# Attention with decay and a gated convolution network on one core: the decay rows on other DMA queues, and a new order for the first half of the program

## The chip, the core and the metric

The kernel runs on one core of a Trainium2 chip. The metric is device time in microseconds, the median of several executions. One further execution was recorded by the hardware profiler; lines and durations come from it. A core has five engines that run side by side, each with an instruction queue of its own: PE (TensorE, matrix products; PEld is its loading of weights), DVE (VectorE), ACT (ScalarE), POOL (GpSimd) and SP (SyncE, which here only issues transfers). SP, ACT and POOL can each issue DMA transfers. An engine takes its instructions strictly in order and waits on semaphores for the others.

## The reference

Two steps follow each other. The first is causal attention with a forget gate, for 8 batches of 8 heads, 576 places, head size 64:

```python
scores = scale * np.matmul(q, k.transpose(0, 1, 3, 2))
cum = np.cumsum(np.log(np.clip(f, 0.0001, 1.0)), axis=-1)
decay = cum[:, :, :, None] - cum[:, :, None, :]
scores = np.where(causal, -1000000000.0, scores + decay)
attn = np.exp(scores - np.max(scores, axis=-1, keepdims=True))
attn = attn / (np.sum(attn, axis=-1, keepdims=True) + 1e-09)
return np.matmul(attn, v).astype(np.float32)
```

Its output, 576 x 512 for each batch, goes through a network with a gate from a convolution over three neighbouring places:

```python
h = np.maximum(x @ w_in, 0.0)                      # 512 -> 1024
conv_out += conv_w[k][None, None, :] * hp[:, k:k + S, :]   # k = 0, 1, 2
gate = 1.0 / (1.0 + np.exp(-conv_out))
return (h * gate @ w_out).astype(np.float32)       # 1024 -> 512
```

## The kernel before

**Tiling.** The work is cut into 16 half batches (hb, four heads each) for the attention and 8 batches (b) for the network. A half batch has two pairs of heads, i = 2 hb and 2 hb + 1. Half batches 0 and 1 are loaded plainly and turned on PE; from half batch 2 on a DMA transpose writes q and k into one of four ring buffers (`qk`).

**The decay on the scores.** Of each float32 number of q and k a bfloat16 half is used, and the other, even rows of a transposed buffer are free. The decay stands there: a row of -cum / scale beside rows of ones, so that the score product adds the difference itself. For that the decay is computed once (`kc`), written to a DRAM tile (`image`), and copied from there into the even rows of each ring buffer, one row on the q side (line 204, 4.5 KB) and two on the k side (line 205, 9 KB). Half batch 0 doesn't use the image: it adds the decay with two further products from `kc` (lines 317 and 319). From half batch 8 on, another function (`fill`) copies four rows at a time from SP. Ahead of the copy for half batches 2 to 7, a "clamp" on DVE (line 186) clears the even rows.

**Tasks.** The program is a list of 1054 named tasks. A string, `ORDER`, fixes the sequence in which they are emitted, and so the order of each engine's queue; where a task may go to several engines, the string names one after an @. The names that matter here:

- `ld`, `q`, `v`: loads of q and k, and of v, by SP. `wi`, `wo`: loads of the weights by SP; `wic`, `woc`: their cast to fp16. `va`: the cast of v.
- `dca`, `dcl`, `dcs`, `dck`: clip, logarithm, running sum, and the rows `kc` of the decay. `ki`: the image in DRAM (line 281, three DMAs). `cw`, `cwt`: the convolution's weights turned on PE, and their ratios on DVE.
- `tp hb.p.side`: q (side 0) or k (side 1) of a pair turned on PE; `cl`: the move out of PSUM (lines 172 and 174), or the clamp from half batch 2 on. `rw hb`: the copy of the image's rows.
- `sd i`, `so i.s`, `st hb`: scores on the diagonal, off it, and of the last 64 places, on PE; `ed`, `eo`, `et`: their exponentials on ACT (lines 355, 372, 334).
- `pv`: the product with v on PE; `n`, `m`: normalisation on DVE (405, 407); `t`, `tx`: the turn of the result on PE (416) and its copy (419).
- `f b.ff`: the network's first product on PE (431); `r`: relu on ACT (442); `c`, `d`: the convolution on DVE (448, 450); `a`: the gate's function on ACT (453); `g`: the gate on DVE (460); `o b.c`: the second product on PE (476); `e`, `s`: its copy and store.

**What the tasks share.** Four PSUM buffers of 128 x 1024 floats hold whatever PE writes; a task that writes one takes the buffer that has been free longest, and its reader on ACT or DVE gives it back. Each engine waits at the head of its queue, so a task that can't start holds everything behind it on that engine.

**Queues.** All transfers but the loads of `f` and `conv_w` and two of the row copies go through SP. SP issues them in order, and each waits on SP until its inputs are there.

Of the kernel before, what the change touches and what calls it, by code (L numbers as in the profile page):

```python
# [21 lines left out]
class Plan:  # L22
# [8 lines left out]
    def add(self, name, engines, after, fn, take=(), give=(), behind=()):  # L31
        assert name not in self.tasks
        self.tasks[name] = dict(engines=engines.split("/"), after=[a for a in after if a], fn=fn, take=list(take),
                                give=list(give), behind=[a for a in behind if a])
        return name
# [21 lines left out]
def kernel(  # L57
# [11 lines left out]
    nc = tc.nc  # L69
# [5 lines left out]
    BH = B * H  # L75
# [70 lines left out]
    add = plan.add  # L146
# [53 lines left out]
    def rows_of(hb, e="SP"):  # L200
        dma = {"SP": nc.sync, "ACT": nc.scalar}[e].dma_start
        h0 = 2 * PAIRS if hb == 0 else 0
        c = slice(hb * HH + h0, (hb + 1) * HH)
        dma(even_rows(hb, 0, 1, h0 * S, HS), image[0:1, 0, c, :].rearrange("j h s -> j (h s)"))
        dma(even_rows(hb, 1, 2, HS + h0 * S, 2 * HS), image[1:3, 1, c, :].rearrange("j h s -> j (h s)"))
# [73 lines left out]
    def decay_image(e):  # L279
        for j, a, h in ((0, 0, 0), (1, 1, 0), (2, 1, 1)):  # L280
            {"SP": nc.sync, "ACT": nc.scalar}[e].dma_start(image[j, a], kc[BH * h:BH * (h + 1)])
# [232 lines left out]
    def stage_cast(w, j, e):  # L514
# [5 lines left out]
        {"ACT": nc.scalar.copy, "POOL": nc.gpsimd.tensor_copy, "DVE": nc.vector.tensor_copy}[e](dst, ob)  # L520

    add("cw", "PE", [], conv_weights, take=["ps"])
    add("cwt", "DVE", ["cw"], conv_ratios, give=[("ps", "cw")])
    for x in range(0):
        add(f"wu{x}", "PE", [], lambda x=x: warm_up(f"wu{x}"), take=["ps"])
        add(f"wd{x}", "PE", [], lambda: None, behind=[f"wu{x}"], give=[("ps", f"wu{x}")])
    add("zc", "SP", [], constants)
    add("dca", "DVE", [], lambda: nc.vector.tensor_scalar(fsb, fsb, 1e-4, 1.0, op0=ALU.max, op1=ALU.min))
    add("dcl", "ACT", ["dca"], decay_log)
    add("dcs", "DVE", ["dcl"], decay_sum)  # L530
    add("dck", "DVE", ["dcs"], decay_rows)
    add("ki", "ACT/SP", ["dck"], decay_image)
    for w in ("wi", "wo"):
        for j in range(4):
            add(f"{w}{j}", "SP", [], lambda w=w, j=j: stage(w, j), take=["ob"])
            add(f"{w}c{j}", "POOL/ACT/DVE", [f"{w}{j}"], lambda e, w=w, j=j: stage_cast(w, j, e), give=[("ob", f"{w}{j}")])

    for hb in range(NHB):
        b = hb // 2
        was = hb - RING  # L540
        old = [f"st{was}"] + [f"sd{2 * was + y}" for y in range(2)] + [
            f"so{2 * was + y}.{s}" for y in range(2) for s in range(2)] if was >= 0 else []
        if hb < NPL:
            parts = [(p, side) for p in range(2) for side in range(2)]
# [13 lines left out]
            if hb == 0:  # L558
                ready = [["dck"] + [f"cl0.{p}.{side}" for side in range(2)] for p in range(2)]
                if PAIRS < 2:  # L560
                    add("rw0", "SP", ["cl0.1.0", "cl0.1.1", "ki"] + ([] if PAIRS else ["cl0.0.0", "cl0.0.1"]), lambda: rows_of(0))
                    ready = [ready[p] if p < PAIRS else ["rw0"] for p in range(2)]
            else:
                add(f"rw{hb}", "ACT/SP", [f"cl{hb}.{p}.{side}" for p, side in parts] + ["ki"], lambda e, hb=hb: rows_of(hb, e))
                ready = [[f"rw{hb}"]] * 2
# [127 lines left out]
```

## Time and profile before

| | |
|---|---|
| median of 3 executions | 245.96 us (245.56 to 246.7) |
| profiled execution | 247.66 us |
| its span, first to last instruction | 245.9 us |
| granted TensorE clock, mean | 0.999 |
| instructions in the span | 6391 |
| read from HBM, written to HBM | 21.11 MB, 10.17 MB |

The busy shares and the chain of waits are shown with the prediction. A row of a time line gives start and length in microseconds, the engine ("SPq" or "ACTq" is a DMA being issued by that engine's queue), the line of the kernel, the operation, and the tile written and the tiles read; in brackets stands how long the engine was idle before, and what ended that.

### The profile page before, as it was taken

Reading aid. Unit: us, or ns where it says so; the run is one execution under the profiler, and the core shown is the slowest. Engines: PE = TensorE matmul, PEld = TensorE weight load, DVE = VectorE, ACT = ScalarE, POOL = GpSimd, SP = SyncE. Lnnn points to the kernel's source line nnn. Section 1 sums busy time; section 2 is a strip of 40 time slices with the busy share of each in tenths; the row PEclk is TensorE's granted clock in tenths of the full one; section 3 lists DMA queues with packets and bytes.
Section 4 is the critical chain, followed back from the end, with each engine's and each line's share of the span. In section 5 each row is a group of like instructions: output and inputs, shape, how many; then the busy total and the mean of one; then the engine's idle time right before and its main releaser. Section 6 shows DMA issues by size and latency. Waiting matters only on the chain.

```text
span 245.9 us, 6391 instructions
## 1 busy us (share of the span) xinstructions
PE 229.1 (93%) x2627; PEld 146.5 (60%) x2627; DVE 205.7 (84%) x323; ACT 207.2 (84%) x278; POOL 52.6 (21%) x77
## 2 busy tenths in 40 slices
PE   0899899959999999999999999999999999999992
PEld 0778676537655776666556865685576557444440
DVE  5626329899999899999999988996999889999951
ACT  2748695999999889999999999999988997698452
POOL 8020430004240030004130481156303131000000
PEclk9999999999999999999999999999999999999999
DMA  6999799999999899999989999929999780551426
GB/s 202 329 154 231 242 189 206 219 201 325 225 203 191 198 196 219 234 301 212 234 248 249 177 191 283 263 48 187 272 245 197 185 192 4 129 176 50 171 87 213
DMA packets 120280, 49.68 MB, mean 202 GB/s; under 512 B 109863, under 2 KB 110375, under 8 KB 120251
## 3 DMA queue, kind: packets, MB, share of 16 engines
q1 hardware_dynamic: 120073, 48.94, 89.1%
q8 instruction: 20, 0.33, 0.6%
q10 hardware_dynamic: 178, 0.34, 0.5%
q14 instruction: 9, 0.07, 0.1%
HBM read 21.11 MB, written 10.17 MB: 127 GB/s over the span
## 4 chain that ended last, share of the span: by engine, by line
PE 79%; DVE 7%; DMA 5%; ACT 5%; issue 1%; SPq 1%; ACTq 0%; DVEq 0%
PE ps L476 25%; PE ps L431 24%; PE ps L314 15%; PE ps L391 7%; DMA qk<-image 3%; DMA u<-in_f_dram 2%; PE ps L396 2%; PE ps L416 2%; PE ps L322 2%; ACT qk L172 2%; DVE xm L407 2%; DVE u L448 1%; DVE u L450 1%; PE ps L317 1%; PE ps L319 1%
## 5 line engine op out<-in xcount | busy, mean ns | idle before, releaser
L431 PE MATMUL ps<-xt,w_in_f 128*128 128x512 f16 (+1 forms) x512 | 70.1, 287 | 0.4 <-DVE xt L419 0.4
L372 ACT ACTIVATE pp<-ps 128x1024 f16<-128x1024 f32 x64 | 64.6, 1030 | 4.1 <-PE ps L314 2.3
L476 PE MATMUL ps<-w_out_f,hg 128*128 128x512 f16 x288 | 66.8, 380 | 0.0
L314 PE MATMUL ps<-qk 128*128 128x128 bf16 (+2 forms) x576 | 64.8, 242 | 1.3 <-ACT pp L355 0.7
L448 DVE SCALAR_TENSOR_TENSOR u<-ht,cwt 128x576 f32<-128x576 f16 x64 | 54.0, 860 | 3.9 <-ACT ht L442 3.6
L453 ACT ACTIVATE hg<-u,cw 128x576 f16<-128x576 f32 x64 | 48.6, 781 | 6.1 <-DVE u L450 6.0
L450 DVE SCALAR_TENSOR_TENSOR u<-ht,cwt,u 128x576 f32<-128x576 f16 x64 | 52.9, 841 | 0.5
L431 PEld LDWEIGHTS <-w_in_f 128*128 128x128 f16 x512 | 34.3, 98 | 28.7 <-issue 0.5
L314 PEld LDWEIGHTS <-qk 128*128 128x128 bf16 x576 | 39.7, 98 | 19.5 <-issue 3.5
L442 ACT ACTIVATE ht<-ps 128x576 f16<-128x576 f32 x64 | 40.9, 661 | 6.4 <-PE ps L431 3.0
L476 PEld LDWEIGHTS <-hg 128*128 128x128 f16 x288 | 26.9, 98 | 28.9
L460 DVE SCALAR_TENSOR_TENSOR hg<-hg,ht 128x576 f16<-128x576 f16 x51 | 38.8, 773 | 0.5 <-ACT hg L453 0.5
L358 POOL TENSOR_SCALAR_AFFINE_SELECT pp<-pd 128x1024 f16<-128x1024 f32 x16 | 19.7, 1245 | 54.2 <-ACT pd L355 54.2
L391 PE MATMUL ps<-va,pp 128*128 128x65 f16 x640 | 24.8, 193 | 1.7 <-DVE va L219 1.7
L391 PEld LDWEIGHTS <-pp 128*128 128x128 f16 x640 | 22.6, 97 | 4.2 <-DVE va L219 2.0
L407 DVE TENSOR_TENSOR xm<-ps,rc 128x896 f16<-128x896 f32 (+1 forms) x32 | 23.9, 752 | 0.5
L355 ACT ACTIVATE pp<-ps 128x1024 f16<-128x1024 f32 x16 | 16.5, 1034 | 5.8 <-PE ps L314 3.3
L355 ACT ACTIVATE pd<-ps 128x1024 f32<-128x1024 f32 x16 | 16.2, 1023 | 1.2 <-PE ps L314 0.5
L219 POOL CAST va<-vf 128x1024 f16<-128x1024 f32 x8 | 9.9, 1233 | 32.6 <-DVE u L448 18.3
L322 PE MATMUL ps<-mask,ident 128*128 128x512 bf16 (+1 forms) x40 | 14.8, 370 | 1.4 <-ACT pp L372 0.8
L405 DVE RECIPROCAL rc<-ps 128x14 f32<-128x14 f32 (+1 forms) x32 | 6.7, 209 | 10.1 <-PE ps L396 4.9
L481 ACT COPY ob<-ps 128x1024 f32<-128x1024 f32 (+1 forms) x14 | 12.9, 918 | 0.3 <-issue 0.2
(83 smaller groups left out, 180.2 us busy)
## 6 DMA issues: line engine op xcount, KB each, us to landing
vf<-in_v_dram SPq DMA_DIRECT2D x32, 256.0 KB
out_dram<-ob SPq DMA_DIRECT2D x14, 512.0 KB
qk<-blank SPq DMA_DIRECT2D x8, 432.0 KB
ob<-in_moe_w_in_dram SPq DMA_DIRECT2D x4, 512.0 KB
ob<-in_moe_w_out_dram SPq DMA_DIRECT2D x4, 512.0 KB
out_dram<-ob SPq DMA_DIRECT2D x6, 256.0 KB
vf<-in_v_dram SPq DMA_DIRECT2D x8, 128.0 KB
qk<-blank SPq DMA_DIRECT2D x8, 108.0 KB
```

What stands on the lines that cost most here:

```text
L314: nc.tensor.matmul(o, tk[:, h * S + k0:h * S + k0 + 128], tq[:, h * S + q0:h * S + q0 + n], start=first, stop=last and not by_matmul(hb, h))
L355: nc.scalar.activation(o, ps_of(f"sd{i}").rearrange("p (s c) -> p s c", s=2), AF.Exp, scale=SCALE)
L372: nc.scalar.activation(pair(i)[:, s, 512:1536], ps_of(f"so{i}.{s}"), AF.Exp, scale=SCALE)
L391: nc.tensor.matmul(ps[:, c:c + D + 1], block(hb, h, m, n), va[:, h, m, 0:D + 1], start=(m == 0), stop=(m == n))
L407: nc.vector.tensor_tensor(xm[:, CUT * D * u:CUT * D * u + nj * k * D].rearrange("p (j x d) -> p j x d", x=k, d=D), got[:, :, :, 0:D], r.un ...
L431: nc.tensor.matmul(ps[:, t0:t1], w_in_f16[:, cc, 128 * ff:128 * (ff + 1)], xt[:, cc // 2, x:x + t1 - t0], start=(cc == 0), stop=(cc == NCC ...
L442: nc.scalar.activation(ht_of(b, ff)[:, 2:2 + S], ps_of(f"f{b}.{ff}")[:, 0:S], AF.Relu, scale=1.0 if (b, ff) in LATE else 0.5)
L448: nc.vector.scalar_tensor_tensor(u, ht[:, 1:1 + S], cwt[:, ff, 0:1], ht[:, 2:2 + S], op0=ALU.mult, op1=ALU.add)
L450: nc.vector.scalar_tensor_tensor(u, ht[:, 3:3 + S], cwt[:, ff, 1:2], u, op0=ALU.mult, op1=ALU.add)
L453: nc.scalar.activation(hg_of(b, ff), u_t[slot[f"c{b}.{ff}", "u"]], AF.Sigmoid if (b, ff) in LATE else AF.Tanh, scale=cw[:, ff, 1:2])
L460: nc.vector.scalar_tensor_tensor(hv, hv, 1.0, ht_of(b, ff)[:, 2:2 + S], op0=ALU.add, op1=ALU.mult)
L476: nc.tensor.matmul(ps[:, 512 * (c % 2):512 * (c % 2 + 1)], w, w_out_f16[:, ff, :], start=(ff == 0), stop=(ff == NFF - 1))
```

## The change

It has two parts.

**Engines.** `decay_image` and `rows_of` may now be issued by POOL as well, and the order names the issuer: the image by POOL (before by SP), the rows of half batches 1 and 3 by ACT (before by SP), those of 2, 4, 5, 6 and 7 by POOL (before 4 and 5 by ACT, the others by SP). Some casts and copies change their engine as well:

| tasks | before | now |
|---|---|---|
| va0.0, va6.0 | POOL | DVE |
| va4.0 | ACT | DVE |
| wic0, wic2, wic3 | POOL | DVE |
| e0.1 | ACT | DVE |
| va1.1, va2.0, tx0, tx4 | DVE | ACT |
| va3.0, va3.1, va5.1, va7.1, va8.0 | ACT | POOL |
| va4.1 | DVE | POOL |
| cl1.0.0 / cl1.0.1 | ACT / DVE | DVE / ACT |

**Order.** The first 500 of the 1054 places of `ORDER` are in a new sequence; from place 501 (`va9.0`) on it is word for word as before. SP's own loads keep their sequence; those tasks that left SP are simply gone from it.

```diff
-dca cw ld0 ld1 ld0.0.0 tp0.0.0 dcl ld0.1.0 ld0.0.1 tp0.0.1 tp0.1.0 v0.0 ld0.1.1 ld1.0.1 ld1.0.0 dcs dck v0.1 v0.2 v0.3 v0.4 va0.0@POOL ki@SP
...
+dca cw dcl ld0 ld1 ld0.0.0 ld0.1.0 tp0.0.0 ld0.0.1 tp0.0.1 v0.0 ld0.1.1 cwt ld1.0.1 dcs cl0.0.1@ACT tp0.1.0 dck ld1.0.0 cl0.0.0@ACT v0.1 ki@POOL
...
     def rows_of(hb, e="SP"):
-        dma = {"SP": nc.sync, "ACT": nc.scalar}[e].dma_start
+        dma = {"SP": nc.sync, "ACT": nc.scalar, "POOL": nc.gpsimd}[e].dma_start
...
     def decay_image(e):
         for j, a, h in ((0, 0, 0), (1, 1, 0), (2, 1, 1)):
-            {"SP": nc.sync, "ACT": nc.scalar}[e].dma_start(image[j, a], kc[BH * h:BH * (h + 1)])
+            {"SP": nc.sync, "ACT": nc.scalar, "POOL": nc.gpsimd}[e].dma_start(image[j, a], kc[BH * h:BH * (h + 1)])
...
-    add("ki", "ACT/SP", ["dck"], decay_image)
+    add("ki", "ACT/SP/POOL", ["dck"], decay_image)
...
-                add(f"rw{hb}", "ACT/SP", [f"cl{hb}.{p}.{side}" for p, side in parts] + ["ki"], lambda e, hb=hb: rows_of(hb, e))
+                add(f"rw{hb}", "ACT/SP/POOL", [f"cl{hb}.{p}.{side}" for p, side in parts] + ["ki"], lambda e, hb=hb: rows_of(hb, e))
...
-                add(f"rw{hb}", "ACT/SP", [f"cl{hb}.{side}" for side in range(2)] + ["ki"], lambda e, hb=hb: rows_of(hb, e))
+                add(f"rw{hb}", "ACT/SP/POOL", [f"cl{hb}.{side}" for side in range(2)] + ["ki"], lambda e, hb=hb: rows_of(hb, e))
```

What this does to the queues is seen at three places. First ACT, from the first exponential on, before (qk_85 and qk_86 are the ring buffers of half batches 0 and 1, pp_95 to pp_98 take the exponentials of pairs; L172 is the move of a turned q or k, L355 and L372 exponentials):

```order
L355 ACTIVATE pp_95<-ps_131 128x2x512
L372 ACTIVATE pp_95<-ps_132 128x1024
L372 ACTIVATE pp_95<-ps_131 128x1024
L172 ACTIVATE qk_86<-ps_129,lim 128x1152
L355 ACTIVATE pp_96<-ps_132 128x2x512
L172 ACTIVATE qk_86<-ps_129,lim 128x1152
L372 ACTIVATE pp_96<-ps_130 128x1024
```

The same place of ACT now:

```order
L355 ACTIVATE pp_95<-ps_131 128x2x512
L172 ACTIVATE qk_86<-ps_132,lim 128x1152 x2
L204 DMA qk_86<-image 1x2304
L205 DMA qk_86<-image 2x2304
L372 ACTIVATE pp_96<-ps_130 128x1024
L355 ACTIVATE pp_96<-ps_129 128x2x512
L372 ACTIVATE pp_96<-ps_131 128x1024
L372 ACTIVATE pp_95<-ps_132 128x1024
L372 ACTIVATE pp_95<-ps_130 128x1024
```

Both moves of half batch 1 now stand ahead of the five large exponentials of half batch 0 that are left, and its row copy, which waits for them and for DVE's share of the moves, stands in the middle of ACT's queue.

Second SP, from half batch 2's second transpose on, before (ob_125 to ob_128 take the four parts of the first weight, qk_88 is half batch 3's buffer):

```order
L180 DMA_TRANSPOSE qk_87<-in_q_dram 128x2304
L512 DMA ob_125<-in_moe_w_in_dram 128x2x512
L204 DMA qk_86<-image 1x2304
L205 DMA qk_86<-image 2x2304
L512 DMA ob_126<-in_moe_w_in_dram 128x2x512
L512 DMA ob_127<-in_moe_w_in_dram 128x2x512
L512 DMA ob_128<-in_moe_w_in_dram 128x2x512
L204 DMA qk_87<-image 1x2304
L205 DMA qk_87<-image 2x2304
L180 DMA_TRANSPOSE qk_88<-in_q_dram 128x2304
```

Third POOL, from its first task after the fills on, as it is now:

```order
L281 DMA image<-kc 64x576 x3
L219 CAST va_92<-vf_89 128x4x4x64
L221 CAST va_91<-vf_89 64x4x64
L204 DMA qk_87<-image 1x16x144
L205 DMA qk_87<-image 2x2304
L520 CAST w_in_f_69<-ob_125 128x2x512
L221 CAST va_93<-vf_90 64x4x64
L219 CAST va_94<-vf_90 128x4x4x64
L221 CAST va_94<-vf_90 64x4x64
L204 DMA qk_85<-image 1x16x144
L205 DMA qk_85<-image 2x2304
```

On SP the row copies between the weights, each of which waited for a move or a clamp, are gone. On POOL the copies of half batch 2 and, further down, of half batch 4 stand among the casts of v and of the weights; the one-row copy is built there as 16 pieces of 144 numbers.

2 lines of the change are left out of this document (1 added, 1 removed).

## The prediction

> **What bounds the kernel now.** I read the page first: the busy shares and the chain that ended last.
>
> ```profile
> PE 229.1 (93%) x2627; PEld 146.5 (60%) x2627; DVE 205.7 (84%) x323; ACT 207.2 (84%) x278; POOL 52.6 (21%) x77
> PE 79%; DVE 7%; DMA 5%; ACT 5%; issue 1%; SPq 1%; ACTq 0%; DVEq 0%
> ```
>
> PE is the bound, but a share is a mean over stages. So next I read the busy time of each engine in stretches (start:end, length, then PE, PEld, DVE, ACT, POOL, the granted clock, DMA share, GB/s).
>
> ```profile
> 6.75:16.00 9.25, 8.58 (x73) 7.71 (x73) 5.58 (x12) 5.68 (x5) 0.00 (x0) 1.00 1.02 279
> 16.00:27.00 11.00, 11.00 (x136) 8.56 (x135) 4.72 (x5) 8.80 (x9) 2.53 (x4) 1.00 0.89 177
> 27.00:40.00 13.00, 11.72 (x204) 8.95 (x201) 5.70 (x11) 9.20 (x11) 3.98 (x4) 1.00 1.10 219
> 40.00:50.00 10.00, 9.27 (x82) 5.40 (x80) 9.03 (x13) 8.68 (x13) 0.39 (x1) 1.00 1.16 231
> 50.00:60.00 10.00, 7.43 (x145) 5.76 (x147) 9.97 (x17) 9.65 (x15) 1.52 (x1) 1.00 1.12 265
> 60.00:120.00 60.00, 59.77 (x719) 38.38 (x718) 57.93 (x86) 57.57 (x79) 9.97 (x9) 1.00 1.09 221
> 120.00:220.00 100.00, 100.00 (x1170) 61.98 (x1168) 92.57 (x136) 92.44 (x128) 28.78 (x28) 1.00 0.84 190
> ```
>
> From 60 to 220 us PE is idle for 0.23 us. Between 27 and 60 it is idle for 13 - 11.72 = 1.28, 0.73 and 2.57 us, together 4.6. The order is unchanged from its 501st place on, and that place lies in the stretch in which PE is full. So the change can win at most about what PE loses before 60 us, and a lead won there is kept to the end as long as DVE and ACT, themselves at 96% from 60 to 120 us, carry it.
>
> What does PE wait for between 16 and 52 us? The time line of ACT (start, length, line, tiles; in brackets the idle time ahead and who ended it) shows two engines that feed each other through four PSUM buffers:
>
> ```profile
> 17.76 1.02 ACT L372 ACTIVATE pp<-ps 128x1024 f16<-128x1024 f32 x1 [0.62 <-PE ps L319]
> 19.58 1.02 ACT L372 ACTIVATE pp<-ps 128x1024 f16<-128x1024 f32 x1 [0.79 <-PE ps L319]
> 20.50 1.30 ACT L172 ACTIVATE qk<-ps,lim 128x1152 uint16<-128x1152 uint16 x1
> 25.48 1.02 ACT L372 ACTIVATE pp<-ps 128x1024 f16<-128x1024 f32 x1 [0.29 <-PE ps L319]
> 26.83 0.38 ACT L334 ACTIVATE pt<-ps 128x256 f16<-128x256 f32 x1 [0.33 <-PE ps L319]
> 28.71 1.02 ACT L355 ACTIVATE pp<-ps 128x1024 f16<-128x1024 f32 x1 [1.49 <-PE ps L314]
> 36.08 1.02 ACT L372 ACTIVATE pp<-ps 128x1024 f16<-128x1024 f32 x1 [0.41 <-PE ps L314]
> 38.25 1.02 ACT L355 ACTIVATE pp<-ps 128x1024 f16<-128x1024 f32 x1 [1.15 <-PE ps L314]
> 40.26 0.65 ACT L442 ACTIVATE ht<-ps 128x576 f16<-128x576 f32 x1 [0.98 <-PE ps L431]
> 41.67 0.65 ACT L442 ACTIVATE ht<-ps 128x576 f16<-128x576 f32 x1 [0.77 <-PE ps L431]
> 49.22 0.65 ACT L442 ACTIVATE ht<-ps 128x576 f16<-128x576 f32 x1 [0.30 <-DVE hg L460]
> ```
>
> The ten gaps add up to 7.1 us. Each buffer of scores needs 1.02 us of ACT and is held until then, so a gap of ACT is lost and comes back as PE's wait for a buffer. The early stage is bound by how well ACT is fed; that is what the new order must change.
>
> **The DMA edits.** SP keeps its other transfers in their order. It loses the image's three and two each for half batches 1, 2, 3, 6 and 7; what they cost now is the time in which SP waits for a clamp with weights queued behind it, and their landing:
>
> ```profile
> 24.46 0.69 SPq L205 DMA_DIRECT2D qk<-image  x1
> 27.10 0.59 SPq L205 DMA_DIRECT2D qk<-image  x1
> 27.10 6.63 DMA qk<-image
> 27.63 0.38 PE L322 MATMUL ps<-mask,ident 128*128 128x512 bf16 x1
> ```
>
> The rows of half batch 1 are issued until 25.15 and used at 27.63 without a wait: at most 2.5 us. Those of half batch 2, behind three weight loads, are issued until 27.69 and landed at 33.73: 6.0 us. PE waits for them at 33.7 with 0.15 us or less, so on their own they are worth nearly nothing. The weights and the next transposes are issued earlier, by the image's three issues at least; DMA is at 0.89 to 1.16 of its time from 16 us on, so they land perhaps 1 us earlier. I cost that at nothing, because the clamps of half batch 3 wait on DVE behind the first transposed outputs anyway.
>
> The Trainium skill, "DMA: Bandwidth & Descriptors", section "Issuing engines are not separate DMA queues", says that transfers issued from several engines end on the same 16 engines, so that spreading them saves only issue time. By that rule half batch 2 would still need something like the 6.0 us; the sum is the same by either, as the rows are wanted about 9 us after their clamp (below).
>
> The price of a row DMA on ACT depends on whether ACT is working when it is issued:
>
> ```profile
> 53.19 1.03 ACT L355 ACTIVATE pp<-ps 128x1024 f16<-128x1024 f32 x1
> 53.51 0.23 ACTq L204 DMA_DIRECT2D qk<-image  x1
> 53.78 0.66 ACTq L205 DMA_DIRECT2D qk<-image  x1
> ```
>
> Those two were issued under a running activation: nothing. Half batch 3 on ACT falls into such a full place: nothing. Half batch 1 does not, since it waits for the move just ahead of it on ACT: 0.23 + 0.66 = 0.9 us of ACT uncovered. No row shows a DMA issued by POOL. Its 13 issues are bounded by 0.23 us, the cheapest issue on a queue, and by POOL's longest cast here, 1.5 us; I take 1 us each, nearer to the casts, as POOL must do work for it. That is 13 us on an engine that is idle for 79% of the span; it shows only where a row lands late (a rival below).
>
> **The order, up to 27 us.** On DVE the seven small instructions of the convolution ratios now stand ahead of the scan.
>
> ```profile
> 10.55 0.76 DVE L276 SCALAR_TENSOR_TENSOR kc<-u,kc 64x576 bf16<-64x576 f32 x1
> 11.34 0.18 DVE L299 COPY cw<-ps 128x24 f32<-128x24 f32 x1
> 12.50 0.17 DVE L306 TENSOR_TENSOR cwt<-cw,cwt 128x8 f32<-128x8 f32 x1
> 19.88 0.38 PE L322 MATMUL ps<-mask,ident 128*128 128x512 bf16 x1
> 21.65 1.17 PE L166 MATMUL ps<-ident_b,hg 128*128 128x128 bf16 x18
> ```
>
> They take 1.3 us, of which some 0.7 fill DVE's wait for the logarithm, so the decay rows come at about 11.9 instead of 11.3. The first scores need them, and need the two moves of ACT that end at about 12.5: hidden, and without that cover it would be 0.6 us. Scores of pair 0 then end at 15.9 as before.
>
> Behind them PE now runs the transposes of half batch 1 (0.6 us each, half of the 1.17) to 17.1, scores of pair 1 (19.88 to 21.65, 1.8 us) to 18.9, two more transposes to 20.05. ACT does ed0 (to 17.1) and one move of 1.30 (to 18.45), and its next in order is the move of the last transpose: **idle 1.6 us**, and then the uncovered row DMA, **0.9**. From 22.3 on ACT has the five large exponentials left of half batch 0 and those of pairs 2 and 3 queued without a gap: PE is ahead of it by then, and half batch 1's rows are wanted at 25.3, 3.0 us after their issue, against the 2.5 above.
>
> **27 to 52 us.** PE stays ahead of ACT: st2 and so4.0 now stand ahead of f0.0, and so4.0, so4.1 and ed4 keep ACT busy where it had gaps of 0.98 and 0.77. ACT's relu takes 0.65 us, a group of f0 about 1.0 on PE (f0.0 and f0.1 stand ahead of the gaps of 0.98 and 0.77 above), so where two relus follow each other some 0.3 are left, twice at most: **0.5**. ACT's idle time becomes 1.6 + 0.9 + 0.5 = 3.0 us for 7.1.
>
> Against it stands work that changes engines, priced by these:
>
> ```profile
> 26.82 1.04 POOL L219 CAST va<-vf 128x1024 f16<-128x1024 f32 x1
> 38.76 0.76 DVE L419 COPY xt<-ps 128x1152 f16<-128x1152 f16 x1 [0.46 <-PE ps L416]
> 50.50 0.69 DVE L219 CAST va<-vf 128x1024 f16<-128x1024 f32 x1
> 51.57 1.06 ACT L219 CAST va<-vf 128x1024 f16<-128x1024 f32 x1
> 59.83 1.12 ACT L419 COPY xt<-ps 128x1152 f16<-128x1152 f16 x1
> 78.35 1.00 ACT L481 COPY ob<-ps 128x1024 f32<-128x1024 f32 x1
> ```
>
> ACT takes tx0 (1.12) and va1.1 (a 256-column piece, 0.38 as at 26.83); va2.0 comes and va3.0 goes at 1.06 each. **ACT's lead at 52 us: 7.1 - 3.0 - 1.5 = 2.6 us.**
>
> DVE takes va0.0 and three weight casts, all before 40 us, where it is idle for 7.3 of 13 us. From the first convolution on it gains 0.3 (f0.0 ready that much earlier), 0.69 (va2.0 goes) and a part of the 0.97 us that it is idle from 40 to 50: **DVE's lead at 52 us: between 1.0 and 2.0, and I take 1.3**, as it must still follow ACT's relus.
>
> **52 us to the end of the change.** All three are full here. ACT gets lighter (va3.1, va4.0, va5.1 and e0.1 go, tx4 comes). DVE gets va4.0 and va6.0 (0.69 each) and e0.1 (1.00, if as on ACT) for tx4 (0.76) and va4.1: +1.3 to +1.6, against 60 - 57.93 = 2.1 us of idle time from 60 to 120 us, which cover it; without that cover it would eat the whole lead of DVE.
>
> The sum therefore lies between DVE's 1.3 and ACT's 2.6. PE follows whichever is later in each place; I take the middle, **1.9 us**. The profiled execution took 247.66 us (span 245.9) and would take 245.8; it is 1.7 above the median of 245.96, and I take the same 1.9 off the median: **244.1 us**.
>
> **Rivals.** (0.5% is about what a measurement of this kernel can tell from no change, 1.2 us: 244.7 to 247.2.)
>
> *The lead is spent on DVE: 245.9.* DVE has 0.03 us free from 50 to 60 us and takes more work than it gives. If its lead at 52 us is 1.0 and the extra 1.3 falls into its full places, nothing is left: 245.96 + 0.3 - 0.3. For it: DVE's 96%; against: the 2.1 us of gaps. Range 245.2 to 246.9.
>
> *PE loses almost nothing before 60 us: 241.9.* Of its 4.6 us idle 0.5 stays. For it: the order was changed at every place where PE waits; against: ACT, which works 36.4 - 7.1 = 29.3 us between 16.1 and 52.5, would have to lose no more than 1.5 us there with its new work, and the two waits of 1.6 and 0.9 are in its order.
>
> *Rows issued by POOL land late: slower, 247.6.* One mechanism: the rows of half batches 4 and 5 wait on POOL behind casts and issue slowly. Those of half batch 4 can be issued when their clamp ends, at about 53 us, and are used where PE had them before:
>
> ```profile
> 60.41 0.39 PE L322 MATMUL ps<-mask,ident 128*128 128x512 bf16 x1
> 58.34 1.52 POOL L520 CAST w_out_f<-ob 128x1024 f16<-128x1024 f32 x1 [13.32 <-DMA ob<-in_moe_w_out_dram]
> ```
>
> That leaves about 7 us; the slowest row DMA above needs 6.0, and half batch 2's rows have some 9. From 7 us on each further microsecond costs one; from 9 the lead is gone; at 10.5 the time is 244.1 + 3.5 = 247.6. For it: a POOL cast took 1.52 us at 58 us beside a full DVE and 1.04 at 26.8, so POOL is slowed by half there. Against: even 1.5 us for each of two issues and 2.5 to land make 5.5.
>
> The Trainium skill, "SBUF — State Buffer", section "SBUF: two separate sides", speaks against the change: descriptors of a DMA issued by GpSimd cannot be written while DVE runs an instruction in a two-port mode, and a transfer of about 620 ns alone took about 3100 ns beside such a copy. By it the two issues would be an estimated 6.2 us and the rows about 1.7 us late. I give it no more than the rival's chance, since the slowed cast is the only row here that agrees with it.
>
> **How the numbers follow.** Forecast (243.3 to 244.7): 0.48. Lead spent on DVE: 0.27. Nearly all of PE's idle time gone: 0.12. Late rows: 0.13. The range from 242.0 to 247.2 takes in the forecast, the first rival, half of the second and the mild part of the last. Faster by over 0.5%: 0.48 + 0.12 less the edge, 0.58; within: 0.28; slower: 0.14.
>
> **What would show it.** Right: ACT's gaps between 16 and 52 us add up to about 3 us, with one of some 1.6 at 18.5 and one at 21.4; PE's idle time from 27 to 60 us falls from 4.6 to about 2.7; f0.7 and sd9 start about 2 us earlier; PE is full from 60 us on. Wrong: PE or ACT waiting for the image after 40 us (the rows from POOL), DVE gaps that vanish while PE has new waits for DVE between 60 and 120 us, or a first exponential of half batch 1 that waits for rows issued by ACT.

## The result and the profile after

| | before | changed |
|---|---|---|
| median | 246.33 us (4 runs, 245.56 to 249.16) | 252.45 us (4 runs, 252.16 to 253.84) |
| profiled execution | 247.66 us | 252.5 us |
| its span | 245.9 us | 250.8 us |
| granted TensorE clock, mean | 0.999 | 0.989 |

The changed kernel is **slower**: ratio 1.0251, 95% interval [1.0215, 1.0286], 6.1 us. The forecast was 244.1 us, the range 242.0 to 247.2. (The kernel of before has a fourth execution here, of 249.16 us, which moves its median from 245.96 to 246.33.)

The page of the changed kernel has the same busy PE and a shorter share of it in the chain that ended last: 68% where it was 79%, and DVE 12% where it was 7%.

```profile
PE 229.1 (91%) x2627; PEld 145.9 (58%) x2627; DVE 211.3 (84%) x325; ACT 206.0 (82%) x275; POOL 60.0 (24%) x91
PE 68%; DVE 12%; DMA 7%; ACT 6%; issue 2%; SPq 1%; ACTq 1%; DVEq 0%
```

Busy time by stretch of the changed kernel (start:end, length, then PE, PEld, DVE, ACT, POOL, granted clock, DMA share, GB/s):

```profile
6.75:16.00 9.25, 8.23 (x91) 7.52 (x92) 6.11 (x13) 6.79 (x7) 1.85 (x4) 1.00 1.19 303
16.00:27.00 11.00, 10.46 (x119) 7.77 (x118) 5.30 (x6) 8.37 (x9) 3.36 (x5) 1.00 1.07 254
27.00:40.00 13.00, 12.92 (x220) 9.97 (x220) 7.51 (x15) 12.17 (x16) 0.00 (x0) 1.00 1.23 213
40.00:50.00 10.00, 8.47 (x93) 5.22 (x92) 9.86 (x13) 8.83 (x14) 3.15 (x3) 1.00 1.28 203
50.00:60.00 10.00, 8.14 (x155) 5.98 (x152) 9.82 (x18) 8.91 (x12) 2.06 (x3) 1.00 1.13 261
60.00:70.00 10.00, 7.38 (x69) 4.22 (x67) 10.00 (x10) 6.79 (x10) 6.12 (x7) 1.00 1.06 195
70.00:80.00 10.00, 9.92 (x91) 6.22 (x91) 9.19 (x14) 8.70 (x13) 0.51 (x1) 0.83 1.07 205
120.00:140.00 20.00, 18.56 (x188) 10.67 (x186) 19.89 (x28) 17.54 (x26) 4.89 (x5) 1.00 0.88 211
140.00:220.00 80.00, 80.00 (x977) 50.34 (x974) 73.11 (x110) 72.96 (x101) 24.91 (x25) 1.00 0.78 177
```

PE's idle time up to 60 us, stretch by stretch, is 1.02, 0.54, 0.08, 1.53 and 1.86 us, together 5.0; before it was 0.67, 0, 1.28, 0.73 and 2.57, together 5.25. So **nearly nothing was won there**. From 27 to 60 us, the stretch of the forecast, it fell from 4.6 to 3.5 us and not to 2.7, and 0.54 us came up ahead of it. New losses stand where PE had been full: 2.62 us from 60 to 70, a clock of 0.83 from 70 to 80 (17% of 10 us, 1.7 us), and 1.44 us from 120 to 140.

PE's waits of the changed kernel, summed (us in total, times, longest):

```profile
PE ps L322 <- ACT ht L442: 2.7, 1, 2.7
PE ps L314 <- DMA qk<-image: 2.6, 3, 1.1
PE ps L314 <- ACT ht L442: 1.8, 3, 0.8
```

The second row is the rows of the image, for which PE waited 0.15 us before. The three waits on PE's time line, one each for half batches 1, 3 and 4:

```profile
24.63 0.40 PE L314 MATMUL ps<-qk 128*128 128x128 bf16 x4 [0.55 <-DMA qk<-image]
45.61 0.38 PE L314 MATMUL ps<-qk 128*128 128x128 bf16 x4 [1.09 <-DMA qk<-image]
59.23 0.40 PE L314 MATMUL ps<-qk 128*128 128x128 bf16 x4 [0.95 <-DMA qk<-image]
```

The first row of the summed waits is one event. Rows of POOL, DVE, ACT and PE around it, in the changed kernel:

```profile
60.40 0.81 DVE L448 SCALAR_TENSOR_TENSOR u<-ht,cwt 128x576 f32<-128x576 f16 x1
...
63.57 0.64 POOL L221 CAST va<-vf 64x256 f16<-64x256 f32 x1 [1.51 <-DMA vf<-in_v_dram]
64.15 2.03 POOL L520 CAST w_out_f<-ob 128x1024 f16<-128x1024 f32 x2
66.13 1.04 POOL L219 CAST va<-vf 128x1024 f16<-128x1024 f32 x1
67.18 1.50 POOL L520 CAST w_out_f<-ob 128x1024 f16<-128x1024 f32 x1
...
63.94 3.84 DVE L448 SCALAR_TENSOR_TENSOR u<-ht,cwt 128x576 f32<-128x576 f16 x1
67.70 2.25 DVE L460 SCALAR_TENSOR_TENSOR hg<-hg,ht 128x576 f16<-128x576 f16 x2
...
69.38 0.65 ACT L442 ACTIVATE ht<-ps 128x576 f16<-128x576 f32 x1 [2.82 <-DVE hg L460]
...
70.08 0.27 PE L322 MATMUL ps<-mask,ident 128*128 128x256 bf16 x1 [2.70 <-ACT ht L442]
72.22 0.63 PE L322 MATMUL ps<-mask,ident 128*128 128x512 bf16 x1
```

Five casts follow each other on POOL without a break from 63.57 to 68.68. The DVE instruction that begins at 63.94 takes 3.84 us; the same form took 0.81 at 60.40. ACT waits for the gate behind it, PE for ACT, and then PE runs at half rate: the product of 0.38 us takes 0.63 at 72.22. An idle time of that length doesn't always bring the half rate: in the kernel e7 below PE was idle for 3.24 us at the same place, and the clock column stayed at 1.00.

The loss between 120 and 140 us stands just behind the 500th place, where the order is as before:

```profile
124.77 3.17 POOL L358 TENSOR_SCALAR_AFFINE_SELECT pp<-pd 128x1024 f16<-128x1024 f32 x2
...
125.45 3.10 DVE L450 SCALAR_TENSOR_TENSOR u<-ht,cwt,u 128x576 f32<-128x576 f16 x2
128.47 0.75 DVE L460 SCALAR_TENSOR_TENSOR hg<-hg,ht 128x576 f16<-128x576 f16 x1
...
132.89 0.65 ACT L442 ACTIVATE ht<-ps 128x576 f16<-128x576 f32 x1 [2.07 <-DVE hg L460]
```

**The sum of the two spans.** PE's idle time up to 60 us -0.2, from 60 to 80 +2.6, from 80 to 120 -0.2, from 120 to 140 +1.4, the clock +1.7; the last copy starts 5.2 us before the end where it started 4.1 before it, +1.1. And the profiled execution of before had a slow start: -1.6, from these rows of PE (before, then changed):

```profile
12.89 0.31 PE L314 MATMUL ps<-qk 128*128 128x128 bf16 x1
13.00 0.31 PE L317 MATMUL ps<-sel_k,kc 128*128 128x128 bf16 x1
```

```profile
13.13 0.22 PE L314 MATMUL ps<-qk 128*128 128x128 bf16 x1 [0.26 <-ACT qk L172]
13.19 0.22 PE L317 MATMUL ps<-sel_k,kc 128*128 128x128 bf16 x1
```

In the profile of before a product of 128 columns began every 0.107 us, and the slow steps went on until about 16.4; in that of the changed kernel it began every 0.055 us from 13.1 on. That is some 3.3 us longer at half rate, half of which is lost; the clock column (1.00 in both) doesn't show it. Together 4.8 of the 4.9 us. The Trainium skill, "TensorE: Matmul & The Clock Gate", section "Part 1: The HAM clock gate (the "warmup" mystery)", says that the array has two rates, and that where the first change falls differs from run to run; the 0.107 and 0.055 agree.

### The profile page after: what moved, and what is told of

Same layout as the page of the kernel before. It is cut to its first block, busy times and chain, and to the rows that moved or that the text cites. A ratio compares the mean times of both kernels' runs of the same rounds, so it can differ in the third digit from the quotient of the medians.

```text
span 250.8 us, 6420 instructions
## 1 busy us (share of the span) xinstructions
PE 229.1 (91%) x2627; PEld 145.9 (58%) x2627; DVE 211.3 (84%) x325; ACT 206.0 (82%) x275; POOL 60.0 (24%) x91
## 4 chain that ended last, share of the span: by engine, by line
PE 68%; DVE 12%; DMA 7%; ACT 6%; issue 2%; SPq 1%; ACTq 1%; DVEq 0%
PE ps L476 22%; PE ps L431 17%; PE ps L314 13%; PE ps L391 7%; DVE u L448 4%; DMA qk<-image 4%; DVE hg L460 3%; PE ps L396 2%; ACT pp L372 2%; DVE u L450 2%; DMA pd<-in_moe_conv_w_dram 2%; PE ps L322 2%; DMA vf<-in_v_dram 2%; PE ps L166 1%; PE ps L416 1%
## 5 line engine op out<-in xcount | busy, mean ns | idle before, releaser
L431 PE MATMUL ps<-xt,w_in_f 128*128 128x512 f16 (+1 forms) x512 | 69.2, 286 | 0.0
L372 ACT ACTIVATE pp<-ps 128x1024 f16<-128x1024 f32 x64 | 64.4, 1037 | 5.3 <-PE ps L314 4.3
L448 DVE SCALAR_TENSOR_TENSOR u<-ht,cwt 128x576 f32<-128x576 f16 x64 | 56.9, 905 | 3.0 <-ACT ht L442 2.7
L450 DVE SCALAR_TENSOR_TENSOR u<-ht,cwt,u 128x576 f32<-128x576 f16 x64 | 53.6, 855 | 0.7
L460 DVE SCALAR_TENSOR_TENSOR hg<-hg,ht 128x576 f16<-128x576 f16 x51 | 39.4, 784 | 1.2 <-ACT hg L453 1.1
L391 PE MATMUL ps<-va,pp 128*128 128x65 f16 x640 | 25.1, 193 | 0.9 <-ACT va L219 0.4
L355 ACT ACTIVATE pp<-ps 128x1024 f16<-128x1024 f32 x16 | 16.5, 1035 | 1.6 <-PE ps L314 1.0
L355 ACT ACTIVATE pd<-ps 128x1024 f32<-128x1024 f32 x16 | 16.3, 1023 | 1.3 <-PE ps L314 0.5
L481 ACT COPY ob<-ps 128x1024 f32<-128x1024 f32 (+1 forms) x13 | 11.8, 911 | 0.9 <-PE ps L476 0.7
```

Of the source, the lines that this page charges most:

```text
L355: nc.scalar.activation(o, ps_of(f"sd{i}").rearrange("p (s c) -> p s c", s=2), AF.Exp, scale=SCALE)
L372: nc.scalar.activation(pair(i)[:, s, 512:1536], ps_of(f"so{i}.{s}"), AF.Exp, scale=SCALE)
L391: nc.tensor.matmul(ps[:, c:c + D + 1], block(hb, h, m, n), va[:, h, m, 0:D + 1], start=(m == 0), stop=(m == n))
L431: nc.tensor.matmul(ps[:, t0:t1], w_in_f16[:, cc, 128 * ff:128 * (ff + 1)], xt[:, cc // 2, x:x + t1 - t0], start=(cc == 0), stop=(cc == NCC ...
L448: nc.vector.scalar_tensor_tensor(u, ht[:, 1:1 + S], cwt[:, ff, 0:1], ht[:, 2:2 + S], op0=ALU.mult, op1=ALU.add)
L450: nc.vector.scalar_tensor_tensor(u, ht[:, 3:3 + S], cwt[:, ff, 1:2], u, op0=ALU.mult, op1=ALU.add)
```

## The experiments

Theories at first: **A**, the unbroken casts on POOL hold DVE. **B**, POOL as the issuer makes rows late. **C**, the order is bad as such. The first three experiments gave **D**: a row copy on SP held SP back until its clamp was done, so that bulk loads behind it didn't fill the DMA engines ahead of the row. Diffs below are of the order's words. Each ratio is to the kernel of before as measured beside that experiment (medians of 245.6 to 246.6 us), so ratios compare better than microseconds.

**e1_rows_act.** The changed kernel, with ki and rw2, rw4 to rw7 issued by ACT:

```diff
-ki@POOL rw2@POOL rw4@POOL rw5@POOL rw6@POOL rw7@POOL
+ki@ACT rw2@ACT rw4@ACT rw5@ACT rw6@ACT rw7@ACT
```

> The new order, but with no DMA issued by POOL: the image and the rows of half batches 2, 4, 5, 6 and 7 are issued by ACT at the same places of the order; POOL's casts stay. Three theories. (A) The burst: five casts back to back on POOL at 63.6 to 68.7 us hold a DVE instruction with two SBUF inputs for 3.8 us, and that starves ACT and PE (2.7 us idle, and half clock after it, 1.7 us). By A this run still has the burst and one L448 of over 3 us, and takes 251 to 253 us, at most 1 us less for the late rows of half batch 4 (0.95 us of waiting). (B) DMAs issued by POOL are the cause (slow issue, late rows, and the longer end of the program, 1.1 us): then this run loses the 5 to 6 us and takes 246 to 248. (C) The order as such: 252 to 253.

Measured 270.24 us, ratio to before 1.1 [1.0953, 1.1048], far above what any of the three expected. PE waited 11.0 us for the image, in five waits. B as first put falls: without POOL the rows are later still.

**e2_burst_act.** The changed kernel with two of the five casts on ACT:

```diff
-woc0@POOL woc1@POOL
+woc0@ACT woc1@ACT
```

> The change with one difference: the casts woc0 and woc1 are done by ACT instead of POOL, which breaks the burst of five casts into pieces; POOL still issues its DMAs. (A) the burst: no L448 above 1.7 us between 60 and 72, PE's 2.7 us of idle time there and the stretch at half clock are gone, time 247.5 to 249.5 (ACT has 3 us free from 60 to 90 us for the two casts). (B) POOL's DMAs: 251.5 to 253. (C) the order as such: 252 to 253.

Measured 253.37 us (250.53 to 254.73), 1.0328 [1.0272, 1.0383]. In its profile PE was full from 60 to 70 us and the half rate was gone, but PE then waited 1.8 us for a weight that ACT had cast. The median speaks against A's 247.5 to 249.5; what speaks for A is that the loss left its place. One thing more shows in this profile, whose order and issuers are those of the changed kernel up to 60 us: PE waited for the rows of half batch 4 alone (0.80 us), not for those of 1 and 3. So how late these rows come differs from one execution to the next.

**e3_issuers.** The order of before with the issuers of the changed kernel:

```diff
-ki@SP rw1@SP rw2@SP rw3@SP rw4@ACT rw5@ACT rw6@SP rw7@SP
+ki@POOL rw1@ACT rw2@POOL rw3@ACT rw4@POOL rw5@POOL rw6@POOL rw7@POOL
```

> The order of before with the issuers of the change: image by POOL, rows of 1 and 3 by ACT, rows of 2 and 4 to 7 by POOL; casts stay on their engines of before. (A) the burst: no burst is made, so 245.5 to 247, as before or up to 0.5% off. (B) POOL's DMAs are the cause: 249 or more, with PE or ACT waiting for the image between 30 and 90 us and an end of the program that is longer by about 1 us. (C) order: as before, 245.5 to 246.7.

Measured 262.16 us, 1.0659 [1.0594, 1.0724]: **the issuers alone cost 16 us**, and the new order wins most of it back. PE's largest wait, 7.6 us, was for the rows of half batch 1.

**e4_rows_sp.** The new order with the old issuers; on SP the image and the rows stand among the loads at places like those of before, and some loads move with them:

```diff
-ki@POOL rw1@ACT rw2@POOL rw3@ACT rw4@POOL rw5@POOL rw6@POOL rw7@POOL
+ki@SP rw1@SP rw2@SP rw3@SP rw4@ACT rw5@ACT rw6@SP rw7@SP
```

> The changed order with the issuers of before: the image and the rows of half batches 1, 2, 3, 6 and 7 on SP, at places among the loads like those of before, 4 and 5 on ACT, no DMA on POOL. Theory D (a row copy on SP held SP back until its move or clamp was done, so that the bulk loads behind it did not yet fill the DMA engines; on another queue the rows share the engines with bulk that was issued early and land 4 to 8 us after their issue): the rows of half batch 1 land within 3 us of their issue, PE's waits for the image fall below 0.5 us, and the time lies near 247 to 250 us, as the run of five POOL casts at 63 us stays where it is and keeps its 2 us. Theory B (GpSimd as the issuer is the cost): also 247 to 250, the two part in the next kernels. Theory C (the new order is at fault with any issuer): 251 or more.

Measured 252.57 us, 1.0273 [1.0205, 1.0341]: as slow as the changed kernel, above the 247 to 250 of B and D and in the range of C (251 or more). PE waited 5.4 us for the image, 3.5 of it for half batch 4, whose rows ACT issued only at 56.2, behind its other work. With the old issuers too the new order wants rows earlier than they come.

**e5_rw1_act** and **e11_sp_held.** The kernel of before with one row copy moved; then the same with SP held back by another:

```diff
-wi1 ... rw1@SP ... wi0 wi2 wi3 ... rw2@SP
+wi1 ... rw1@ACT ... wi0 wi2 wi3 ... rw2@SP      (e5)
+wi1 ... rw1@ACT ... rw2@SP wi0 wi2 wi3          (e11)
```

In e11 the cast `wic0` on POOL moves along with its weight.

> The kernel of before with one edit: the two row copies of half batch 1 are issued by ACT at their place, where they stood on SP; everything else, the other rows on SP too, is as before. Theory D: SP no longer stops behind the first weight load, issues the other three weights and what follows 2 to 4 us earlier, and the rows land 5 us or more after their issue where they needed 2.5; PE waits 3 to 6 us for them near 27 us and the time is 248 to 252 us. Theory B, and the prediction's own costing: ACT pays 0.9 us of issue at most, 246 to 247 us.

> The kernel of e5 (before, with the rows of half batch 1 issued by ACT) with SP held back in another way: on SP the rows of half batch 2, which wait for their clamps, stand ahead of the second, third and fourth weight instead of behind them. ACT still issues the rows of half batch 1. Theory D (what makes the rows late is the bulk that SP has issued ahead of them, not the engine that issues them): the rows of half batch 1 land within 3.5 us of their issue instead of 5.1, PE's wait for them falls from 4.4 us to 2 or less, and the time is 246.5 to 250 us against 254.16, less what the later weights cost. Rival (a row copy issued by ACT is slow as such): the landing still takes 5 us and the time is 253 us or more.

e5 measured 254.16 us, 1.0325 [1.0292, 1.0359]: one row copy, 8.4 us. Of these PE's wait is 4.4, and two stretches at half rate lose 3.4 (clock 0.87 over the 13 us from 27 and 0.83 over the 10 us from 50). e11 measured 249.93 us, 1.0139 [1.0051, 1.0227]. The time lines of e5 (the issue on ACT, four weights on SP, PE's wait):

```profile
25.60 0.23 ACTq L204 DMA_DIRECT2D qk<-image  x1
25.95 0.66 ACTq L205 DMA_DIRECT2D qk<-image  x1
...
21.05 2.71 SPq L512 DMA_DIRECT2D ob<-in_moe_w_in_dram  x4
...
31.07 0.61 PE L314 MATMUL ps<-qk 128*128 128x128 bf16 x4 [4.43 <-DMA qk<-image]
```

and of e11:

```profile
25.26 0.69 ACTq L205 DMA_DIRECT2D qk<-image  x1
...
21.17 0.59 SPq L512 DMA_DIRECT2D ob<-in_moe_w_in_dram  x1
25.70 2.31 SPq L512 DMA_DIRECT2D ob<-in_moe_w_in_dram  x3
...
27.47 0.40 PE L314 MATMUL ps<-qk 128*128 128x128 bf16 x4 [1.47 <-DMA qk<-image]
```

The same issuer at the same place, counted from the start of the second issue: 31.07 - 25.95 = 5.1 us to land behind four weights, 27.47 - 25.26 = 2.2 behind one. The next transpose on SP could be a rival to the three weights, since e11 holds it back too. The DMA packets of the two traces decide: in e5 those of the four weights run from 22.5 to 30.0 us with no gap above 0.25 us, nothing else of SP's moves between 22.8 and 28.3, and the three packets of the rows, of 0.18 us each, start at 29.3, 29.8 and 30.0, as the weights run out. In e11 there are no packets of weights from 25.1 to 27.0 us, and those of the rows start at 25.9 and 26.8. D holds for this row copy. ACT as the issuer is not the cost; what SP no longer waits for is.

**e6_rw_pool** and **e13_ki_pool.** The kernel of before with only its later rows, or only its image, on POOL:

```diff
-ki@SP  rw2@SP rw4@ACT rw5@ACT rw6@SP rw7@SP
+ki@SP  rw2@POOL rw4@POOL rw5@POOL rw6@POOL rw7@POOL   (e6)
+ki@POOL  rw2@SP rw4@ACT rw5@ACT rw6@SP rw7@SP         (e13)
```

> The kernel of before with the rows of half batches 2, 4, 5, 6 and 7 issued by POOL at their places; the image and the rows of 1 and 3 stay on SP. Theory B (the issuer GpSimd is the cost): most of the 16 us that the changed issuers cost in the order of before are here, 255 us or more. Theory D: the throttle on SP at half batches 1 and 3 is still there, so the rows of half batch 2 land about as late as before (6 us) and the time is 246 to 250 us; the part above 247 would be casts on POOL that queue behind a row copy, or a row copy behind a cast.

> The kernel of before with one edit: the image's three DMAs are issued by POOL, behind the first cast of v, and no longer by SP. All rows stay as before. Theory G (a program that has had the image written by POOL ends about 1 us later after its last copy): the stretch from the start of the last copy to the end of the span is 5.2 us where it was 4.1, with the old order too, and the time is 246.8 to 248 us. By theory D nothing else is lost, since the rows of half batch 1 on SP still hold SP back. Rival (the later end comes from the new order): 4.1 to 4.6 us at the end, 246 to 246.8 us; or the image lands late behind the cast and PE waits for the rows of half batch 1: a wait for the image of over 1 us near 28 us.

e6 measured 252.61 us, 1.027 [1.0229, 1.031], between what B and D expected: PE waited 3.7 us for half batch 2, whose row copy stood on POOL behind the cast of a weight that was itself still loading. e13 measured 246.57 us, 1.0002 [0.9985, 1.0019]: the image on POOL is free.

**e7_sp_two.** The changed kernel with the rows of half batches 1 and 3 on SP:

```diff
-rw1@ACT ... v0.4 ... q2.1 ... q2.0 ... wi1 ... rw3@ACT
+v0.4 q2.1 q2.0 wi1 rw1@SP ... rw3@SP
```

> The changed kernel with the rows of half batches 1 and 3 alone put back on SP, those of 1 behind the first weight load as before; the image and the other five stay on POOL. Theory D: the rows of half batch 1 land within 3 us instead of 4.4, those of 3 faster than 4.65, PE's waits between 40 and 60 us shrink by 1 to 2 us, and the time is 249 to 251.5 us. Theory B: PE waits as in the changed kernel, 252 us or more.

Measured 250.75 us, 1.0205 [1.0148, 1.0261]: 1.7 us below the changed kernel, but the intervals of the two ratios overlap. PE's one wait for the image is 0.17 us, and its idle time in the five stretches up to 60 us is 0.81 + 0 + 0.08 + 1.02 + 1.15 = 3.1, against 5.25 before. So in this execution, in which the rows came in time, **the order is worth about 2.2 us up to 60 us**. It is the only one: in e8, e9, e12 and e14 below, with the rows of half batches 1 and 3 on SP as here, PE waited 1.8 to 3.3 us for rows (those of half batch 1 on SP, of 2 and 4 on POOL) and was idle for 4.0 to 4.8 us from 16 to 60 us, where it was 2.25 in e7, 4.01 in the changed kernel and 4.58 before. Putting these rows back on SP is therefore not enough. The lines from 16 to 60 us of e7 and e8 (columns as above):

```profile
16.00:60.00 44.00, 41.75 (x600) 30.40 (x598) 33.39 (x50) 39.68 (x51) 8.46 (x11) 1.00 1.17 231
16.00:60.00 44.00, 39.52 (x569) 28.34 (x567) 31.81 (x47) 37.41 (x47) 10.55 (x13) 1.00 1.14 229
```

The burst then takes what e7 had won; rows of its DVE and ACT (of the two gates in the first row one took 0.75 us and the other 4.88):

```profile
63.90 5.56 DVE L460 SCALAR_TENSOR_TENSOR hg<-hg,ht 128x576 f16<-128x576 f16 x2
...
69.55 0.65 ACT L442 ACTIVATE ht<-ps 128x576 f16<-128x576 f32 x1 [3.65 <-DVE hg L460]
```

**e8_spread.** e7 with two of the five casts earlier on POOL:

```diff
-woc3@POOL ... va4.1@POOL ... woc0@POOL ... woc1@POOL ... va5.0@POOL woc2@POOL
+woc3@POOL woc1@POOL woc0@POOL ... va4.1@POOL ... va5.0@POOL woc2@POOL
```

> The kernel of e7 (the changed one with the rows of half batches 1 and 3 on SP) with one edit: on POOL the casts woc1 and woc0 stand straight behind woc3, so that they run near 57 to 60 us, while POOL is idle, and no longer in the unbroken run of five casts at 63 to 69 us. Theory A (while POOL works on from one instruction to the next, a DVE instruction on SBUF operands does not get through and ends with POOL's run; what waits for DVE stops with it): the two L460 that took 5.56 us together at 63.9 take 3 us or less, the fifth relu of batch 1 starts 2 us or more earlier than its 69.55, and the time is 247 to 249.5 us against 250.75. Rival (the gap at 66 to 70 us has another cause, such as the order of the relus): 250 to 251.5 us with the same gap.

Measured 249.64 us, 1.0122 [1.0056, 1.0187], just above A's range. The same two gates in e8 (1.58 and 0.74 us), then the fourth relu of batch 1, which now waits for one of them, and the fifth, which doesn't:

```profile
66.34 2.25 DVE L460 SCALAR_TENSOR_TENSOR hg<-hg,ht 128x576 f16<-128x576 f16 x2
...
68.02 0.65 ACT L442 ACTIVATE ht<-ps 128x576 f16<-128x576 f32 x1 [0.58 <-DVE hg L460]
...
68.83 0.66 ACT L442 ACTIVATE ht<-ps 128x576 f16<-128x576 f32 x1
```

ACT's gap of 3.65 is 0.58, PE's idle time from 60 to 70 us falls from 2.99 to 0.57. A holds for the gap, though the fifth relu came only 0.7 us sooner where 2 were expected: from 16 to 60 us PE had been idle for 4.5 us in this execution and for 2.25 in that of e7, with 2.5 us of waits for rows against 0.17. In time e7 and e8 aren't clear of each other; against the changed kernel the two edits together are (1.0122 [1.0056, 1.0187] for 1.0251 [1.0215, 1.0286]), about half of the loss.

**e10_bunch.** The kernel of before, with the casts put together:

```diff
-woc3@POOL woc1@POOL ... woc0@POOL ... va5.0@POOL ... woc2@POOL
+va5.0@POOL woc3@POOL woc1@POOL woc0@POOL ... woc2@POOL
```

> The kernel of before with one edit on POOL alone: the three casts of the second weight that ran at 58 to 62 us stand behind va5.0, so that five casts follow each other from 67 us on. No other engine's instructions change. Theory A: a DVE instruction that starts in that run takes 3 us or more, PE has a new wait of 2 to 3 us between 68 and 80 us, and the time is 248 to 250 us. Rival (the casts on POOL do not hold DVE, or PE has the slack): 245.5 to 246.5 us.

Measured 250.65 us, 1.0167 [1.0094, 1.0241], above the 248 to 250 of A. POOL and DVE of e10, and PE's wait:

```profile
67.48 6.09 POOL L520 CAST w_out_f<-ob 128x1024 f16<-128x1024 f32 x4
...
68.07 3.09 DVE L450 SCALAR_TENSOR_TENSOR u<-ht,cwt,u 128x576 f32<-128x576 f16 x2
71.08 1.58 DVE L448 SCALAR_TENSOR_TENSOR u<-ht,cwt 128x576 f32<-128x576 f16 x1
...
PE ps L476 <- POOL w_out_f L520: 3.1, 2, 2.6
```

Both sides suffer: every DVE instruction in the run takes about 1.5 us for 0.8, every cast of a weight 1.5 for 1.04. None takes the 3 us or more that A expected: here DVE and POOL take turns, and why DVE had to wait for several casts in the changed kernel and in e7 stays open. PE's loss in e10 is its wait for the late weight itself, so its size says little about A.

**e9_va9_act** and **e12_va9_late.** e8 with the cast just behind the 500th place moved from DVE to ACT, at its place, and then into ACT's gap:

```diff
-va9.0@DVE ... f3.5 ... r3.5 ... r3.6      (e8)
+va9.0@ACT ... f3.5 ... r3.5 ... r3.6      (e9)
+f3.5 ... r3.5 va9.0@ACT ... r3.6          (e12)
```

> The kernel of e8 with one more edit: the cast va9.0, which stands on DVE just behind the 500th place, goes to ACT. Theory F (at the 500th place PE is not behind the kernel of before, but DVE is, by about 2 us of work that the new order has left to it, and PE loses that 2 us as soon as it waits for DVE's gates): the seventh relu of batch 3, which came 2.8 us behind the sixth where it came 0.5 behind it in the kernel of before, moves up by about 0.7, and the time is 0.5 to 1 us below that of e8. Rival (POOL's masks at 121 to 126 us alone make that gap): no difference to e8.

> The kernel of e8 with va9.0 moved from DVE to ACT at a place where ACT has nothing to do: straight behind the sixth relu of batch 3, in the gap of 2.06 us in which it waited for DVE's gate. Theory F (behind the 500th place PE waits for DVE's backlog): the gate comes 0.6 us sooner, the cast fills half the gap, the seventh relu starts 0.6 to 0.95 us sooner after the third than the 8.72 us of e8, and the time is 0.6 to 0.9 us below e8, 248.7 to 249.2 us. Rival (e9 gained 0.3 us there by chance, or the gap is set by something else): 249.6 us or more, with the same 8.7 us.

e9 measured 249.58 us, 1.0108 [1.0028, 1.0188]; e12 249.37, 1.0119 [1.0085, 1.0153]. Counted from r3.3 (which the text on e12 calls the third), the gate comes 0.6 us sooner (7.28 us for 7.88 in e12), as F (PE waits for DVE's backlog there) has it, and r3.6, which waits for it, 0.3 us sooner (8.41 for 8.72). That is what F's mechanism would give, in one profile of each; no gain in time shows, and most of this loss stays.

**e14_ki_sp.** e12 with the image on SP. It tried **theory G**, that the later end comes from the image on POOL:

```diff
-ki@POOL ... v0.4 q2.1
+v0.4 ki@SP q2.1
```

> The kernel of e12 (the new order, rows of half batches 1 and 3 on SP, the weight casts spread, va9.0 on ACT) with the image's three DMAs on SP ahead of the first transpose as in before; the other five rows stay on POOL. Theory G: the end shortens from 5.27 to 4.1 to 4.6 us and the time falls to 248.2 to 248.8 us. Rival: no change at the end, 249 to 249.7 us. It stays above the kernel of before by either.

Measured 249.36 us, 1.0099 [1.0066, 1.0132]: no gain. From the start of the last copy to the end it took 4.6 us, which G wanted, but in e13 4.7 where G wanted 5.2, and neither time follows. G falls as a price of the image.

No version tried beats the kernel of before.

## Why the prediction was wrong

**Wrong first: "I cost that at nothing".** The prediction saw that SP would issue weights and transposes earlier, and that a row copy needed 2.5 us where little was ahead of it and 6.0 behind three weights. It didn't join the two: the waits that it struck from SP were what kept the DMA engines free for the rows. In the changed kernel all four weights were issued by 22.25 us; the rows of half batch 1 landed 3.8 us after the end of their issue where 2.5 were expected (4.4 after the start of the second issue), those of half batch 3 4.65 us after the start of theirs, where nothing was charged. PE's three waits, 2.6 us, are more than the gain of 1.9. e5 and e11 show the mechanism by itself, in the old order. In the new order it is one part: the new order also wants the rows sooner. With half batch 1 back on SP, e8, e9, e12 and e14 still waited 0.61, 0.56, 0.65 and 1.75 us for its rows, and those of half batch 4, issued by POOL, came 0.8 to 1.2 us late in all new orders with POOL but e7. Without its waits for rows PE's idle time from 16 to 60 us would be some 1.4 to 2.3 us in six of the seven kernels with the new order and rows on POOL (3.3 in e2) for the 4.6 of before: the gain that was forecast is about what these waits took. That is a subtraction and no run; only e7 came near to showing it.

**Wrong second: DVE's extra casts "which cover it".** The prediction counted DVE's work against its idle time, 1.3 to 1.6 us against 2.1, with the durations of quiet places. Which of POOL's casts would run together, and beside what, it didn't ask. 0.81 us became 3.84, PE lost 2.6 us and then 1.7 to the half rate. With two of the casts elsewhere the gap closed (e8). It had the hint in hand, a cast of 1.52 us beside a full DVE, and read it as a price for POOL alone. The Trainium skill, "SBUF — State Buffer", section "SBUF: two separate sides", was weighed for its sentence on descriptors; the one that bears on this loss is beside it: a DVE instruction with two SBUF inputs and a GpSimd instruction that reads SBUF exclude each other for a whole instruction. The trace agrees in part: in e10 the two engines take turns, at about 1.5 us an instruction (0.8 and 1.04 alone); the 3.84 and 4.88 us are a wait for several casts, where the rule speaks of one instruction.

**Wrong third: a lead at the 500th place "is kept to the end as long as DVE and ACT ... carry it".** The condition stood in the text and was not worked out for the place where the two orders join. In the changed kernel the relu r3.3 on ACT starts at 124.16 us, in that of before at 122.41. The convolution c3.2 on DVE, the same form in both, follows before and then now at:

```profile
125.46 0.81 DVE L448 SCALAR_TENSOR_TENSOR u<-ht,cwt 128x576 f32<-128x576 f16 x1
```

```profile
129.74 0.81 DVE L448 SCALAR_TENSOR_TENSOR u<-ht,cwt 128x576 f32<-128x576 f16 x1
```

From r3.3 on DVE needs 5.6 us where it needed 3.0, and 5.6 in e8 too: at this place it lags behind ACT, which feeds it. PE loses 1.4 us there. That DVE's backlog costs the 1.4 us is argued from these times; e9 and e12, which took one cast from DVE, left 1.0 and 1.1 of them, and POOL's masks beside DVE (two L450 of 3.10 us for 1.6) are a rival that no run removed.

Two of the signs that the prediction named for a wrong outcome are what the profile shows: PE waiting for the image after 40 us, and a new wait behind DVE between 60 and 120 (through ACT).

**Right.** ACT's gap at 18.5 came at 18.67 with 1.47 us for 1.6, the uncovered row issue at 20.86 with 0.88 for 0.9:

```profile
18.67 1.31 ACT L172 ACTIVATE qk<-ps,lim 128x1152 uint16<-128x1152 uint16 x1 [1.47 <-PE ps L166]
20.86 1.02 ACT L372 ACTIVATE pp<-ps 128x1024 f16<-128x1024 f32 x1 [0.88 <-DVE va L219]
```

(The second row names a cast on DVE as the end of the gap; ACT's own second issue, from 20.16 to 20.81, fills it.)

The eight gaps of ACT from 16 to 52 us add up to 4.5 us for 3.0. Row issues on POOL were priced at 1 us and took 0.51 to 0.52 us for most. The rival of late rows had the right direction for half batch 4, with 0.95 us instead of 3.5, but not its mechanism: the two issues took 0.51 and 0.52 us, and the landing 5.9 us from the start of the second. The larger part was in half batches 1 and 3, on ACT.

**The base.** 1.6 us of what the changed profile seems to lead by in its first 60 us is the slow start of the profiled execution of before. Taking the same difference off the median, as the prediction did, was right; reading leads by a task's time (61.60 to 57.16 for the last normalisation of pair 3) would not have been, since the new order also moves that task ahead of others. PE's idle time doesn't have that fault.

**Open.** The last copy starts 5.2 to 5.3 us before the end in all seven kernels that have both the image and rows on POOL, and 4.1 to 4.7 us before it in all others; the runs show no cause. And the 1.0 to 1.2% that e12 and e14 still lack are only partly named: 1.1 us of idle time behind the 500th place, 1.8 and 2.8 us of waits for rows, and in e12 that later end. Why the rows came in time in e7 and not in e8, whose SP queue is the same, the runs don't show.

## What to carry to other kernels

A wait in a DMA queue may be holding back what stands behind it: before a transfer is moved to another queue, look at what the old queue will issue in its place, and how long the small transfer takes with that in flight. Where an engine takes more work, lay it beside what the others do at that very time, not beside its idle total, and lead PE, DVE and ACT separately over a place where two orders join. Compare two profiles by PE's idle time, after a look at the rate of its first products, and not by one execution each: what e7 won up to 60 us didn't come back in four kernels with the same queue on SP.

## What the runs showed of the hardware

- A copy of three rows (13.5 KB) issued by ACT landed after 2.2 us with one weight of 512 KB issued ahead of it by SP, after 5.1 us with four. Its packets took 0.18 to 0.25 us each and started as those of the weights ran out, though another engine had issued them (e5, e11).
- A DVE instruction on two SBUF tiles took 3.84 us beside five casts of POOL without a break, and 4.88 in e7, for 0.7 to 0.8 alone; the casts went on at 0.64 to 1.5 us. In e10 DVE and POOL took turns, at about 1.5 us for each instruction.
- The issue of a row copy took POOL 0.51 to 0.52 us in nine of ten cases (0.93 once), with 3.6 and 4.0 us from issue to landing (medians).
- PE ran at half rate until about 16.4 us in one execution and 13.1 in another, and again behind the idle 2.70 us, where the clock column shows 0.83 over ten microseconds; at the start the column shows 1.00. Behind an idle time of 3.24 us in e7 it kept its full rate.
